# Issue order around the change of row tiles: a weight split ahead of the next rows' parts, merged quarter transfers, and an earlier turn of old rows

## The chip, the cores and the metric

The kernel runs on one core of one Trainium2 chip. The metric is the device time of one execution in microseconds (us). Engines are named as in the profile: PE is TensorE (matmuls), PEld its weight loads, DVE is VectorE, ACT is ScalarE, POOL is GpSimd, and SP is SyncE, which issues almost all of the DMAs here (SPq is its queue). PSUM is the memory that PE writes its results to, and SBUF the memory that all engines work in.

## What is computed

Eight batches of 576 tokens, eight heads of 64: two attention steps through 32 packed queries, a two-dimensional Fourier transform of which the real part is added, a normalisation, and a two-layer network with a relu. The part around which the change turns is the last one:

```python
p_packed = sm_attn(p, k, v)
x = sm_attn(q, p_packed, p_packed)           # then (8, 576, 512)
u = x + np.real(np.fft.fft(np.fft.fft(x, axis=1), axis=2))
un = (u - mu) / np.sqrt(var + 1e-06)
return u + np.maximum(un @ w_ch1, 0.0) @ w_ch2   # 512 -> 2048 -> 512
```

All is in 32-bit floating point. Each matrix product of the network is made of three matmuls of a faster 32-bit type: every operand is split into a high part (a rounding copy on ACT) and a low part (the rest, a subtraction), and the product is high x high + high x low + low x high.

## The kernel before

**Tiles.** The 4608 rows (8 x 576) are cut into 36 blocks of 128 rows, with the name key: (batch, "E" or "O", 0 or 1), and after each second batch a block of leftover rows "R". Four blocks make a tile of 512 rows, so there are nine tiles, 0 to 8. While the network runs on tile t, `front(t + 1)` computes the rows u of batch t + 1 in small steps between the network's matmuls; its last part ("rest") runs on into steps 0 and 2 of the next tile.

**The network of one tile (`ffn`, L643).** The 2048 hidden units are 16 slices, j = 0 to 15. `up(j)` is 12 matmuls (4 pieces of the inner dimension, three products each) into a PSUM tile ph; ACT then writes hh (relu, high part) and DVE hl (low part). `down(j)` is 12 matmuls (4 row blocks, three products each) which add into four PSUM tiles acc. The loop runs down one slice behind up: up(j), then down(j - 1); down(15) stands after the loop. Here a run of 12 matmuls is called a half step. `step(i)`, called twice a slice (i = 2j and 2j + 1), runs what falls due and the next piece of `front`.

**Weights and their splits.** All weights stay in SBUF (w1f, w2f). Each use splits 128x512 of them anew: `wsplits` (L633) is a generator, and each `next(splits)` issues one split, wr_h on ACT (L101) and wr_l on POOL (L102), and queues it in `ready`. Six buffers "wr" hold three splits. Two are issued in each j: the first is w1[j + 1], the second w2[j]; at j = 15 the first is w2[15], which down(15) reads, the second w1[0] for the next tile; one more, w1[1], follows down(15).

**The rows of the next tile (`Turned`, L581).** up reads the rows transposed and split, in one pair of tiles uh, ul (one buffer each, four quarters of 128 columns). `parts(i)` makes block i's quarter: a copy to uh on ACT and the subtraction to ul on DVE. As there is one buffer, parts can only run when up(15) has ended. At j = 15 parts(0) and parts(1) come behind up(15), parts(2) behind down(14), parts(3) behind down(15); the next up(0) reads all four. In its first slice the four matmuls with ul come last.

The turned rows that parts reads come by one of two ways, for each pair h of blocks (h = 0: blocks 0 and 1, h = 1: blocks 2 and 3), by `kind`:

- "late", where the block is finished too late in this tile: `less` on DVE, and `moves`, eight transposes on PE in among the matmuls of down(14) and down(15).
- "old" (both blocks belong to earlier batches) and "new" (a block of the batch now being computed): `less_quarters` subtracts the mean on ACT (un, L612), `turn` (L616) transposes 32x32 squares on DVE (flip, L619), and 16 DMAs on SP (raw, L623) put the squares in place. Each DMA moves 32 partitions of two blocks: two runs of 128 elements (512 B) a partition. un has two buffers ("ln").

Pairs into tiles 1, 2, 3 are new, late; into tiles 4, 5, 6, 7 old, new; into tile 8 old, old. Before, the first old pair is turned after step 24 (j = 12), and a new pair, or the second of two old pairs, at j = 13 (un behind down(12), the turn after step 27). At the end of a tile four DVE operations (L721) add acc into u, and four DMAs (L722) store it.

**What sets the order.** From tile 1 on (L769), the instructions of PE, DVE, ACT and POOL keep the order in which the program issues them. Tile 0's are ordered by a planner when the program is built, and so is SP's queue in all tiles. Each engine works through its instructions in order.

`statistics` puts squares (ACT, L208), a scalar operation (DVE, L211) and a power (POOL, L212) one and two steps behind a block.

Of the kernel before, what the change touches and what calls it, by code (L numbers as in the profile page):

```python
# [9 lines left out]
F32 = mybir.dt.float32  # L10
# [7 lines left out]
P = 128  # L18
# [61 lines left out]
def tile_kernel(ctx, tc, kpT, qT, v, w1, w2, tabs, tabR, tabB, tabT, sel, ident_d, out):  # L80
    nc = tc.nc
# [3 lines left out]
    ld = ctx.enter_context(tc.tile_pool(name="ld", bufs=2))  # L85
    work = ctx.enter_context(tc.tile_pool(name="work", bufs=2))
# [39 lines left out]
    def load_base():  # L126
        nc.gpsimd.dma_start(basis, tabB)
        nc.sync.dma_start(turn, tabT)
# [452 lines left out]
    class Turned:  # L581
# [32 lines left out]
                                     AF.Identity, bias=stat_of[key][:, 1:2], scale=1.0)  # L614

        def turn(self, h):  # L616
            flip = ld.tile([P, 2, 4, P], F32, tag="ld", name="flip")
            for n in range(2):
                nc.vector.transpose(flip[:, n].rearrange("p q x -> p (q x)"), self.un[2 * h + n])  # L619
            raw = work.tile([P, 2, 4, P], F32, tag="wst", name="raw", bufs=2)  # L620
            for a in range(4):
                for q in range(4):
                    nc.sync.dma_start(raw[32 * q:32 * (q + 1), :, a, :], flip[32 * a:32 * (a + 1), :, q, :])  # L623
            for n in range(2):
                self.tp[2 * h + n] = raw[:, n].rearrange("p q (c k) -> p q c k", c=4)

        def parts(self, i):
            if self.hl is None:
# [4 lines left out]
    def wsplits():  # L633

        for _ in tiles:
            for n, j in [(0, 0)] + [x for j in range(1, NJ) for x in ((0, j), (1, j - 1))] + [(1, NJ - 1)]:
                hi = work.tile([P, DM], F32R, tag="wr", name="wr_h", bufs=6)
                lo = work.tile([P, DM], F32R, tag="wr", name="wr_l", bufs=6)
                split(hi, lo, (w1f, w2f)[n][:, j, :], nc.gpsimd)
                ready.append((hi, lo))  # L640
                yield

    def ffn(first, turned, step, nxt, alone, following):  # L643
        keys = turned.keys
        n = len(keys)
        T = n * P
        uh, ul = turned.hl
        acc = [psf.tile([P, DM], F32, tag=f"acc{i}", name=f"acc{i}") for i in range(n)]
        now["acc"] = acc

        def up(j):
            wh, wl = ready.pop(0)

            pool, tag = (ps, "ps") if alone and j % 2 else (psf, "ph")
            ph = pool.tile([P, 512], F32, tag=tag, name="ph")

            step = T // 2 if first == 0 and j < SPL else T
            order = sorted(range(12), key=lambda k: k % 3 == 1) if j == 0 else range(12)
            for t in (slice(i, i + step) for i in range(0, T, step)):
                for n, k in enumerate(order):  # L660
                    c, (l, r) = k // 3, ((wh, uh), (wh, ul), (wl, uh))[k % 3]
                    nc.tensor.matmul(ph[:, t], l[:, c * P:(c + 1) * P], r[:, c, t], start=(n == 0), stop=(n == 11))  # L662
            hh = work.tile([P, 512], F32R, tag="hh", name="hh")
            hl = work.tile([P, 512], F32R, tag="hl", name="hl")
            nc.scalar.activation(hh[:, :T], ph[:, :T], AF.Relu)  # L665
            nc.vector.scalar_tensor_tensor(hl[:, :T], ph[:, :T], 0.0, hh[:, :T].bitcast(F32), ALU.max, ALU.subtract)  # L666
            return hh, hl

        def down(j, hh, hl, moves=()):

            moves = list(moves)
            vh, vl = ready.pop(0)
            for i in range(n):
                w = slice(i * P, (i + 1) * P)
                for k, (l, r) in enumerate(((hh, vh), (hh, vl), (hl, vh))):
                    nc.tensor.matmul(acc[i], l[:, w], r, start=(j == 0 and k == 0), stop=(j == NJ - 1 and k == 2))  # L676
                    if moves:
                        moves.pop(0)()

        kinds = [nxt.kind(h, following) for h in range(2)] if nxt else []  # L680
        assert kinds in ([], ["new", "late"], ["old", "new"], ["old", "old"]), kinds

        prev = None
        late = "late" in kinds
        for j in range(NJ):
            last = nxt is not None and j == NJ - 1
            cur = up(j)
            if last:
                if late:
                    nxt.less(2)  # L690
                    nxt.less(3)
                nxt.parts(0)
                nxt.parts(1)
            next(splits, None)
            step(2 * j)
            if j == 12:
                if kinds[:1] == ["old"]:
                    nxt.less_quarters(0)
                    nxt.turn(0)
            if prev is not None:  # L700
                down(j - 1, *prev, [lambda: None] * 8 + nxt.moves(2) if last and late else ())
                if j == 13:
                    for h in range(2):
                        if kinds and (h == 1 or kinds[h] != "old") and kinds[h] != "late":
                            nxt.less_quarters(h)
                if last:
                    nxt.parts(2)
                next(splits, None)
            step(2 * j + 1)
            if j == 13:  # L710
                for h in range(2):
                    if kinds and (h == 1 or kinds[h] != "old") and kinds[h] != "late":
                        nxt.turn(h)
            prev = cur
        down(NJ - 1, *prev, nxt.moves(3) if late else ())
        if nxt:
            nxt.parts(3)
        next(splits, None)
        for i, key in enumerate(keys):
            u = u_of[key]  # L720
            nc.vector.scalar_tensor_tensor(u, acc[i], stat_of[key][:, 2:3], u, ALU.mult, ALU.add)  # L721
            nc.sync.dma_start(out[(first + i) * P:(first + i + 1) * P, :], u)  # L722
            free.append(place_of[key])
# [24 lines left out]
    ready, splits = [], wsplits()  # L748
    next(splits)
    next(splits)  # L750
    for t, (first, tk) in enumerate(tiles):

        gen = front(t + 1) if t + 1 < B else iter(())
        ended = []

        def step(i):

            next_step()
            if t > 0 and i in (0, 2):
                next(rest, None)  # L760
            elif not ended and next(gen, None) == "rest":
                ended.append(gen)
            if t == 0 and i % 2 == 0 and i // 2 + LEAD < NJ:
                load_weights(i // 2 + LEAD)
            assert i < 2 * NJ - 1 or t + 1 >= B or ended

        nxt = Turned(tiles[t + 1][1]) if t + 1 < len(tiles) else None

        with tc.manual_schedule(engines=MANUAL) if t > 0 else nullcontext():  # L769
            ffn(first, cur, step, nxt, t + 1 >= B, t + 1)  # L770
        cur, rest = nxt, gen
# [112 lines left out]
```

## Time and profile before

| | us |
|---|---|
| median of three runs (1031.3, 1029.72, 1031.12) | 1031.12 |
| the profiled execution's own time | 1029.28 |
| one raw transfer, issue to landing | 1.9 |
| one copy to uh on ACT, median | 0.616 |
| one subtraction to ul on DVE, median | 0.688 |

The profile is of one execution, which was 1.84 us below the median. The page lists by engine what is busy and what chain of work ended last; "chain" rows called issue are time in which an engine waited for nothing that the profile shows. In a timeline a row gives the start in us, the duration, engine, line, operation, output <- input, and in brackets the idle time before it and what ended that. PE's matmuls are pipelined: a matmul of 512 columns shows 0.39 us, while its successor starts 0.227 us after it at full clock. A granted clock of 1.00 is full speed.

How the sixteen DMAs of a turn stand on SP, in the change from tile 5 to tile 6: first the 32 of both turns, then loads for a later batch.

```profile
704.85 20.82 SPq L623 DMA_DIRECT2D raw<-flip  x32
725.76 1.60 SPq L224 DMA_DIRECT2D kp<-kpT  x2
730.04 2.31 SPq L722 DMA_DIRECT2D out<-ubuf  x4
```

### The profile page before, as it was taken

Reading aid. Unit: us, or ns where it says so; the run is one execution under the profiler, and the core shown is the slowest. Engines: PE = TensorE matmul, PEld = TensorE weight load, DVE = VectorE, ACT = ScalarE, POOL = GpSimd, SP = SyncE. Lnnn points to the kernel's source line nnn. Section 1 sums busy time; section 2 is a strip of 40 time slices with the busy share of each in tenths; the row PEclk is TensorE's granted clock in tenths of the full one; section 3 lists DMA queues with packets and bytes.
Section 4 is the critical chain, followed back from the end, with each engine's and each line's share of the span. In section 5 each row is a group of like instructions: output and inputs, shape, how many; then the busy total and the mean of one; then the engine's idle time right before and its main releaser. Section 6 shows DMA issues by size and latency. Waiting matters only on the chain.

```text
span 1027.5 us, 15015 instructions
## 1 busy us (share of the span) xinstructions
PE 962.4 (94%) x5588; PEld 784.0 (76%) x5588; DVE 578.7 (56%) x1227; ACT 458.5 (45%) x936; POOL 473.6 (46%) x426
## 2 busy tenths in 40 slices
PE   4199889999999999999999999999999999997998
PEld 2177678778877887788777887788778888886886
DVE  4885863669455855587457845694558552122112
ACT  4578634444443444444544454445444442342322
POOL 3715634364345534454445434643454354443443
PEclk9599989999999999999999999999999999998999
DMA  9367301310042002300240024001410020011001
GB/s 361 116 181 269 124 1 45 107 57 1 9 130 71 1 1 86 99 1 1 79 150 1 1 61 139 31 1 28 156 47 1 18 66 1 1 29 54 1 1 41
DMA packets 34825, 65.93 MB, mean 64 GB/s; under 512 B 5494, under 2 KB 19648, under 8 KB 34752
## 3 DMA queue, kind: packets, MB, share of 16 engines
q1 hardware_dynamic: 33776, 63.53, 18.8%
q0 software_dynamic: 976, 1.44, 0.4%
q8 instruction: 44, 0.72, 0.3%
q14 instruction: 29, 0.24, 0.1%
HBM read 48.70 MB, written 9.44 MB: 57 GB/s over the span
## 4 chain that ended last, share of the span: by engine, by line
PE 65%; issue 8%; DVE 8%; SPq 7%; POOL 5%; ACT 4%; DMA 3%; POOLq 0%; ACTq 0%; DVEq 0%
PE ph L662 30%; PE acc L676 25%; SPq L623 7%; POOL wr_l L102 4%; DVE turned L410 1%; DVE turned L406 1%; PE po L317 1%; DMA raw<-flip 1%; PE s L260 1%; DMA wst<-w 1%; PE py L228 1%; PE py L230 1%; PE py L229 1%; PE e1tp L294 1%; DVE flip L619 1%
## 5 line engine op out<-in xcount | busy, mean ns | idle before, releaser
L102 POOL TENSOR_TENSOR wr_l<-w1f,wr_h 128x512 fp32r<-128x512 f32 x144 | 192.7, 1340 | 362.6 <-ACT wr_h L101 358.4
L666 DVE SCALAR_TENSOR_TENSOR hl<-ph,hh 128x512 fp32r<-128x512 f32 x144 | 98.9, 687 | 315.4 <-ACT hh L665 315.0
L102 POOL TENSOR_TENSOR wr_l<-w2f,wr_h 128x512 fp32r<-128x512 f32 x144 | 192.8, 1339 | 118.5 <-ACT wr_h L101 108.4
L662 PE MATMUL ph<-uh,wr_h 128*128 128x512 f32 (+1 forms) x580 | 230.9, 398 | 16.7 <-DVE hl L666 8.8
L676 PE MATMUL acc<-wr_l,hh 128*128 128x512 f32 x576 | 226.2, 393 | 5.8 <-POOL wr_l L102 5.8
L676 PE MATMUL acc<-wr_h,hh 128*128 128x512 f32 x576 | 226.5, 393 | 2.3 <-ACT wr_h L101 1.9
L662 PE MATMUL ph<-uh,wr_l 128*128 128x512 f32 (+1 forms) x580 | 227.5, 393 | 0.9 <-POOL wr_l L102 0.7
L676 PE MATMUL acc<-wr_h,hl 128*128 128x512 f32 x576 | 225.2, 391 | 0.0
L662 PE MATMUL ph<-ul,wr_h 128*128 128x512 f32 (+1 forms) x580 | 222.1, 391 | 0.0
L665 ACT ACTIVATE hh<-ph 128x512 fp32r<-128x512 f32 x144 | 86.0, 597 | 288.0 <-PE ph L662 287.7
L662 PEld LDWEIGHTS ph<-uh,wr_h 128*128 128x128 f32 x580 | 110.1, 190 | 52.3 <-DVE hl L666 10.2
L676 PEld LDWEIGHTS acc<-wr_l,hh 128*128 128x128 f32 x576 | 108.2, 188 | 29.7 <-POOL wr_l L102 8.6
L662 PEld LDWEIGHTS ph<-uh,wr_l 128*128 128x128 f32 x580 | 109.9, 189 | 25.8 <-POOL wr_l L102 2.4
L676 PEld LDWEIGHTS acc<-wr_h,hh 128*128 128x128 f32 x576 | 108.2, 188 | 25.7 <-ACT wr_h L101 3.4
L662 PEld LDWEIGHTS ph<-ul,wr_h 128*128 128x128 f32 x580 | 109.9, 190 | 22.3 <-DVE mx L279 0.8
L676 PEld LDWEIGHTS acc<-wr_h,hl 128*128 128x128 f32 x576 | 108.1, 188 | 22.8
L101 ACT CAST wr_h<-w1f 128x512 fp32r<-128x512 f32 x144 | 88.3, 613 | 10.7 <-PE acc L676 7.2
L101 ACT CAST wr_h<-w2f 128x512 fp32r<-128x512 f32 x144 | 89.1, 619 | 8.3 <-PE ph L662 6.7
L228 PE MATMUL py<-gh,fh 128*128 128x258 f32 x64 | 18.7, 294 | 27.5 <-ACT fh L470 27.5
L208 ACT ACTIVATE junk<-ubuf,stat 128x512 f32<-128x512 f32 x36 | 25.8, 720 | 36.4 <-DVE stat L204 36.4
L102 POOL TENSOR_TENSOR gl<-turned,gh 128x516 fp32r<-128x516 f32 x16 | 25.3, 1582 | 22.9 <-ACT gh L101 22.9
L228 PEld LDWEIGHTS py<-gh,fh 128*128 128x128 f32 x64 | 12.4, 194 | 28.5 <-ACT fh L470 28.0
(201 smaller groups left out, 1291.9 us busy)
## 6 DMA issues: line engine op xcount, KB each, us to landing
kp<-kpT SPq DMA_DIRECT2D x16, 608.0 KB, 4.0
out<-ubuf SPq DMA_DIRECT2D x36, 256.0 KB, 2.1
vt<-v SPq DMA_DIRECT2D x14, 640.0 KB, 4.7
wst<-w SPq DMA_DIRECT2D x17, 512.0 KB, 4.4
qt<-qT SPq DMA_DIRECT2D x14, 576.0 KB, 4.6
raw<-flip SPq DMA_DIRECT2D x208, 32.0 KB, 1.9
ubuf<-w SPq DMA_DIRECT2D x9, 512.0 KB, 3.7
w1f<-w SPq DMA_DIRECT2D x3, 512.0 KB, 14.0
```

Source lines behind the costliest of these rows:

```text
L101: nc.scalar.copy(hi, src)
L102: (lo_eng or nc.vector).tensor_tensor(lo, src, hi.bitcast(F32), ALU.subtract)
L208: nc.scalar.activation(junk, u, AF.Square, bias=st[:, 1:2], scale=1.0, accum_out=st[:, 2:3])
L228: nc.tensor.matmul(o, lh, rh, start=first, stop=False)
L229: nc.tensor.matmul(o, lh, rl, start=False, stop=False)
L230: nc.tensor.matmul(o, ll, rh, start=False, stop=last)
L260: nc.tensor.matmul(res[g][c][at, :w.stop - w.start], lhs(g, h), rhs(g, h, w), start=True, stop=True, tile_position=(r, h * NPK))
L623: nc.sync.dma_start(raw[32 * q:32 * (q + 1), :, a, :], flip[32 * a:32 * (a + 1), :, q, :])
L662: nc.tensor.matmul(ph[:, t], l[:, c * P:(c + 1) * P], r[:, c, t], start=(n == 0), stop=(n == 11))
L665: nc.scalar.activation(hh[:, :T], ph[:, :T], AF.Relu)
L666: nc.vector.scalar_tensor_tensor(hl[:, :T], ph[:, :T], 0.0, hh[:, :T].bitcast(F32), ALU.max, ALU.subtract)
L676: nc.tensor.matmul(acc[i], l[:, w], r, start=(j == 0 and k == 0), stop=(j == NJ - 1 and k == 2))
```

## The change

Three edits. (1) In each j, the first `next(splits)` is called ahead of the parts of the next tile instead of behind them; this makes a difference only at j = 15, where it is the split of w2[15]. (2) flip and raw are laid out with the quarter outside and the block inside, so that one quarter of two blocks is one run of 256 elements (1024 B) a partition in each DMA; there are still 16 DMAs a turn, and DVE writes each transposed block as four pieces. (3) Every old pair is now prepared and turned after step 22 (j = 11): the first old pair of tiles 3 to 7, from step 24; the second of tile 7, from j = 13. For new pairs nothing moves.

```diff
         def turn(self, h):
-            flip = ld.tile([P, 2, 4, P], F32, tag="ld", name="flip")
+            flip = ld.tile([P, 4, 2, P], F32, tag="ld", name="flip")
             for n in range(2):
-                nc.vector.transpose(flip[:, n].rearrange("p q x -> p (q x)"), self.un[2 * h + n])
-            raw = work.tile([P, 2, 4, P], F32, tag="wst", name="raw", bufs=2)
+                nc.vector.transpose(flip[:, :, n, :], self.un[2 * h + n].rearrange("p (q x) -> p q x", q=4))
+            raw = work.tile([P, 4, 2, P], F32, tag="wst", name="raw", bufs=2)
             for a in range(4):
                 for q in range(4):
-                    nc.sync.dma_start(raw[32 * q:32 * (q + 1), :, a, :], flip[32 * a:32 * (a + 1), :, q, :])
+                    nc.sync.dma_start(raw[32 * q:32 * (q + 1), a].rearrange("p n x -> p (n x)"),
+                                      flip[32 * a:32 * (a + 1), q].rearrange("p n x -> p (n x)"))
             for n in range(2):
-                self.tp[2 * h + n] = raw[:, n].rearrange("p q (c k) -> p q c k", c=4)
+                self.tp[2 * h + n] = raw[:, :, n, :].rearrange("p q (c k) -> p q c k", c=4)
...
             cur = up(j)
+            next(splits, None)
             if last:
                 if late:
                     nxt.less(2)
                     nxt.less(3)
                 nxt.parts(0)
                 nxt.parts(1)
-            next(splits, None)
             step(2 * j)
-            if j == 12:
-                if kinds[:1] == ["old"]:
-                    nxt.less_quarters(0)
-                    nxt.turn(0)
+            if j == 11:
+                for h in range(2):
+                    if kinds[h:h + 1] == ["old"]:
+                        nxt.less_quarters(h)
+                        nxt.turn(h)
             if prev is not None:
                 down(j - 1, *prev, [lambda: None] * 8 + nxt.moves(2) if last and late else ())
                 if j == 13:
                     for h in range(2):
-                        if kinds and (h == 1 or kinds[h] != "old") and kinds[h] != "late":
+                        if kinds[h:h + 1] == ["new"]:
                             nxt.less_quarters(h)
...
             if j == 13:
                 for h in range(2):
-                    if kinds and (h == 1 or kinds[h] != "old") and kinds[h] != "late":
+                    if kinds[h:h + 1] == ["new"]:
                         nxt.turn(h)
```

## The prediction

> **What bounds the kernel.** I read the page first, then TensorE's waits, then busy time and clock window by window around each change of tile, then the timelines of ACT, POOL and SP there.
>
> ```profile
> span 1027.5 us, 15015 instructions
> ...
> PE 962.4 (94%) x5588; PEld 784.0 (76%) x5588; DVE 578.7 (56%) x1227; ACT 458.5 (45%) x936; POOL 473.6 (46%) x426
> ...
> PE 65%; issue 8%; DVE 8%; SPq 7%; POOL 5%; ACT 4%; DMA 3%; POOLq 0%; ACTq 0%; DVEq 0%
> ```
>
> TensorE is busy 94% of the span and no other engine over 56%, so only what shortens TensorE's idle or slow time counts. Its longest waits:
>
> ```profile
> PE py L228 <- ACT fh L470: 27.5, 2, 26.0
> PE ph L662 <- DVE hl L666: 8.8, 4, 5.1
> PE ph L662 <- ACT uh L101: 5.9, 4, 4.5
> PE acc L676 <- POOL wr_l L102: 5.8, 7, 0.8
> ```
>
> (total, times, longest.) The first two belong to tile 0, which the change hardly touches. The last two are what it is about: rows of the next tile (uh) that come late, and the remainder of a weight split (wr_l) that comes late at seven changes of tile. I now measure each change. "Change 6-7" is the end of tile 6 and the start of tile 7. Columns: window, length, TensorE busy (instructions, with one or two that reach over an edge), granted clock, DMA share, GB/s.
>
> ```profile
> 179.73:186.13 6.40, 6.40 (x34) 1.00 0.01 4
> 286.90:295.50 8.60, 6.94 (x33) 1.00 0.32 86
> 396.35:405.11 8.76, 6.93 (x34) 1.00 0.28 83
> 505.97:516.63 10.66, 9.06 (x37) 1.00 0.36 108
> 614.74:625.42 10.68, 9.08 (x38) 1.00 0.35 104
> 723.47:733.22 9.75, 8.81 (x38) 1.00 0.67 234
> 831.31:840.60 9.29, 8.46 (x38) 1.00 0.17 57
> 921.89:941.81 19.92, 14.51 (x49) 0.83 0.23 76
> 919.17:921.89 2.72, 2.72 (x13) 1.00 0.22 56
> 928.60:933.10 4.50, 0.01 (x1) 0.93 0.11 29
> 933.10:939.00 5.90, 5.80 (x13) 0.50 0.48 178
> ```
>
> The ninth row is the ruler: a half step (12 matmuls) at full pace takes 2.72 us. Rows 1 to 3 (changes 0-1, 1-2, 2-3) hold down(14), down(15) and eight transposes; rows 4 to 7 hold down(14), down(15) and the next up(0), 3 x 2.72 = 8.16 at full pace; row 8 (change 7-8) holds down(14), down(15), up(0), up(1), 10.88. Change 0-1 stands without a stall, at 6.40. The excess is 8.60 - 6.40 = **2.20**, 8.76 - 6.40 = **2.36**, then **2.50**, **2.52**, **1.59**, **1.13**, and 19.92 - 10.88 = **9.04**: together **21.34 us**. The last two rows show why change 7-8 costs so much: 4.5 us idle, then 5.9 us at half clock.
>
> **The change, part by part.**
>
> *The split ahead of the parts.* ACT at change 7-8, then POOL and TensorE:
>
> ```profile
> 922.09 0.60 ACT L665 ACTIVATE hh<-ph 128x512 fp32r<-128x512 f32 x1 [3.82 <-PE ph L662]
> 922.58 1.13 ACT L101 CAST uh<-raw 128x512 fp32r<-128x512 f32 x2
> 923.62 0.62 ACT L101 CAST wr_h<-w2f 128x512 fp32r<-128x512 f32 x1
> ```
> ```profile
> 924.31 1.46 POOL L102 TENSOR_TENSOR wr_l<-w2f,wr_h 128x512 fp32r<-128x512 f32 x1 [3.92 <-ACT wr_h L101]
> ```
>
> The split of w2[15] stands behind two uh copies, so wr_l ends at 925.77. Down(15) would reach its second matmul, which reads it, at 921.89 + 2.72 + 0.23 = 924.84. Issued first, wr_h starts at 922.58 and wr_l ends about 924.6, in time. In changes 1-2 and 2-3 it is worse, as the uh copies wait for their transfers and hold the split. That the order is what counts, change 0-1 shows, where wr_h was issued ahead:
>
> ```profile
> 177.04 0.62 ACT L101 CAST wr_h<-w2f 128x512 fp32r<-128x512 f32 x1 [1.60 <-PE acc L676]
> ...
> 180.78 1.13 ACT L101 CAST uh<-raw 128x512 fp32r<-128x512 f32 x2
> ```
>
> So this part takes all of 2.20, 2.36 and 1.13, and by the same 1.13 of each of the four others: 5.69 + 4 x 1.13 = **10.2 us**. In return uh0, uh1, their ul, and in changes 1-2 to 6-7 the pow pair on POOL behind them come 0.52 us later; the split takes the wr buffers of w2[13], read out half a step before, so it adds no wait. Next late is then wr_l of w1[0], the pair of POOL instructions being ahead of it:
>
> ```profile
> 509.81 1.06 POOL L212 TENSOR_TENSOR stat<-stat,mhalf 128x1 f32<-128x1 f32 x2
> ```
>
> At change 3-4 I lay it out: uh1 ends 508.3, ul1 509.2, the scalar pair on DVE 509.3, L212 510.4, wr_l (1.3 us) 511.75; up(0) asks for it at 505.97 + 5.44 + 0.23 = 511.64. With its hand-over that is 0.15 us left at each of changes 3-4 to 6-7 (0 to 0.5): **-0.6**. In changes 1-2 and 2-3 the transposes give TensorE 0.9 us more, and nothing is left.
>
> *One run per transfer.* SP's issue durations (ns, least/median/most) of today's two-run transfers and of a load with one run a partition:
>
> ```profile
> L623 SPq DMA_DIRECT2D raw<-flip x208: 585/595/1257, 160.3 to 929.4; - x104
> ```
> ```profile
> L224 SPq DMA_DIRECT2D kp<-kpT x16: 327/334/530, 0.7 to 727.0; - x16
> ```
> ```profile
> 908.88 21.11 SPq L623 DMA_DIRECT2D raw<-flip  x32
> ```
> ```profile
> raw<-flip SPq DMA_DIRECT2D x208, 32.0 KB, 1.9
> ```
>
> 32 issues take 21.11 us, 0.66 each. With one run of 1024 B instead of two of 512 B an issue costs between 0.33 (kp, a load from HBM) and 0.60 us (unchanged), plus 0.06 between issues; I take 0.34, as its pattern is kp's: 16 issues 6.4 us instead of 10.2 to 10.6. DVE's turn writes four pieces instead of one: at most its 0.7 us again, and DVE is under 60% busy. The sum needs this part little, since the next one starts the transfers early enough; what it is worth at the other end stands under rival A. The Trainium skill, "DMA: Bandwidth & Descriptors", Specifications, puts line rate at 512 B a descriptor and above, which the old runs have already: by that rule merging gains nothing in the transfer itself, and only SP's issue time could move.
>
> *Old pairs at step 22.* In tile 7 both old pairs now start at step 22. Today the 32 transfers run from 908.88; the last lands at 931.4, and TensorE stands:
>
> ```profile
> 931.44 0.62 ACT L101 CAST uh<-raw 128x512 fp32r<-128x512 f32 x1 [7.20 <-DMA raw<-flip]
> ```
>
> One loop turn earlier (5.44 us) the first goes out at 903.5, the last at 903.5 + 32 x 0.4 = 916.3, landed by 918.2, before up(15) ends at 921.89. Then uh2 and uh3 run right behind uh1, wr_l of w1[0] is done about 926.6, and up(0) starts at 927.33 without a gap. The half clock goes with the gap: after tile 0's wait of 5.1 us for hl, which ended at 132.88 (second wait row), the clock halves in the same way, while stalls of 1 us (rows 2 to 7 above) leave 1.00:
>
> ```profile
> 132.90:137.00 4.10, 4.10 (x10) 0.50 0.00 0
> ```
>
> Of 9.04 this part gets 7.91 beside the split's 1.13. The slow stretch alone cost 941.81 - 933.15 - 5.44 = 3.2 us. The Trainium skill, "TensorE: Matmul & The Clock Gate", Part 1, gives about 3.4 us of cold pace after an idle window of 3.4 us; by that estimate the slow stretch is 1.7 us and the sum 1.5 smaller. The trace has it longer, and is used.
>
> In tiles 3 to 6 the old pair's turn moves likewise, past nothing on SP but the kp load that stood between the two turns:
>
> ```profile
> 499.03 0.33 SPq L224 DMA_DIRECT2D kp<-kpT  x1
> 499.42 10.48 SPq L623 DMA_DIRECT2D raw<-flip  x16
> ```
> ```profile
> 511.40 0.62 ACT L101 CAST uh<-raw 128x512 fp32r<-128x512 f32 x1 [3.10 <-DMA raw<-flip]
> ```
>
> That load went out only when the first turn had landed, and held the second turn (its flips were done at 497.5) by 1.9 us. Now the first turn has landed before 493. The second runs 497.6 + 16 x 0.4 + 1.9 = 505.9, before uh2 can start (508.2). So the rest of 2.50, 2.52 and 1.59 goes: 1.37 + 1.39 + 0.46 = 3.22.
>
> What the move costs: ACT's two un copies and DVE's flips, each moved ahead of the split of w2[11]:
>
> ```profile
> 906.77 1.34 ACT L612 ACTIVATE un<-ubuf,stat 128x512 f32<-128x512 f32 x2
> ```
> ```profile
> 907.53 1.33 DVE L619 STREAM_TRANSPOSE flip<-un 128x512 f32<-128x512 f32 x2 [0.44 <-ACT un L612]
> ```
> ```profile
> 905.80 0.39 PE L676 MATMUL acc<-wr_l,hh 128*128 128x512 f32 x1
> ```
>
> In tiles 3 to 6 down(11) lies behind other matmuls, over 5 us later: free. In tile 7 four un copies stand there, and the third waits for the first flip (two ln buffers): un from 901.33, third 902.85, fourth to 904.2, wr_h to 904.7, wr_l to 906.1, asked for at 905.80: **-0.3** (0 to 0.6).
>
> **Sum:** 21.34 - 0.6 - 0.3 = 20.4 us. The profiled execution took 1029.28 (span 1027.5): 1008.9. The median shown, 1031.12, lies 1.84 above it: **1010.7 us**.
>
> **Rivals.**
>
> *A, transfers no cheaper to issue.* For it: the two-run and one-run rows differ in more than the runs (SBUF to SBUF against HBM). Then 32 x 0.66 from 903.5 end at 924.6, land at 926.5; uh2, wr_h, wr_l follow to 929.1, 1.2 us after up(0) asks. At 3-4 and 4-5 wr_l of w1[0] moves to 512.2, 0.55 each. Together 2.3: 1013.0.
>
> *B, the gap at 7-8 stays long enough for half clock,* SP holding the second old pair back behind something its planner puts there. Against it: SP has nothing but raw and the final stores in that stretch. 3.2 us for the clock with a gap of 2 or more, up to all 7.9: 1016 to 1018.6.
>
> *C, the split's move does not act,* since POOL or the hh copy is the limit: 10.2 come back, 1020.9. Change 0-1 speaks against it.
>
> *D, slower.* Tile 0 is the one whose order on the engines is planned when the program is built, not written out; the new order and the new transfer shape lie in it. Its plan has a 27.5 us wait for fh already (first wait row). If the new plan makes tile 0 over 20.4 us longer, the whole is slower; a second wait like that one gives 1010.7 + 27.5 = 1038. Against it: the changed instructions stand after 159 us, behind that wait, with 30 us of tile 0 left.
>
> **How the numbers follow.** Forecast 0.66 (own range 1008.5 to 1012.3: the residues from 0 to 2 + 0.6, the runs' spread), A 0.17, B 0.07, C 0.05, D 0.05. The range 1007.5 to 1016.0 takes in the forecast, A and the near end of B. A measurement here tells about 0.2% (2 us) from none. Faster by more than that: forecast, A, B and C, 0.95, less 0.01 for an unforeseen mixture; within 0.2%: 0.02, a D that just cancels; slower: 0.04.
>
> **What would show it.** POOL wr_l and ACT uh gone from TensorE's waits at changes of tile; windows as above at 6.4, 8.2 to 8.4 and 10.9 us; raw issues of about 335 ns; the clock at 1.00 after tile 7; a wait of 0.3 us for wr_l in down(11) of tile 7. I am wrong if a raw issue still takes 0.59 us, if uh waits for raw, if tile 0 lasts longer, or if the pow pair leaves over 0.5 us a change.

## The result, and the profile after

| | before | after |
|---|---|---|
| median of 4 runs (us) | 1031.1 (1029.72 to 1031.3) | 1018.46 (1017.34 to 1019.64) |
| ratio, with its 95% interval | | 0.988 (0.9863 to 0.9898) |
| profiled execution (its span) | 1029.28 (1027.5) | 1017.34 (1015.6) |

The change saves 12.6 us of the 20.4 that were forecast. The time lies 7.8 us above the forecast and 2.5 us above the upper end of the range.

From the page of the kernel after, span, busy times, and the shares of the chain that ended last:

```profile
span 1015.6 us, 15016 instructions
...
PE 957.9 (94%) x5588; PEld 782.3 (77%) x5588; DVE 582.9 (57%) x1227; ACT 459.2 (45%) x936; POOL 474.6 (47%) x426
...
PE 71%; DVE 8%; issue 7%; POOL 5%; ACT 3%; SPq 3%; DMA 2%; DVEq 0%; POOLq 0%; ACTq 0%
```

TensorE still sets the time, and SP's share of the chain fell from 7% to 3%: most of the time that the transfers had on the path is gone, as meant. TensorE's waits after (total, times, longest), of those that belong to changes of tile:

```profile
PE ph L663 <- POOL wr_l L102: 4.6, 5, 1.5
...
PE untp L603 <- DVE un L596: 1.6, 2, 0.8
...
PE ph L663 <- ACT uh L101: 0.5, 1, 0.5
...
PE acc L677 <- POOL wr_l L102: 0.2, 1, 0.2
```

The wait of down for wr_l (5.8 us before) is gone (the 0.2 left is a new place, in tile 7), that of up for uh fell from 5.9 to 0.5. In their place stand two new ones: up waits 4.6 us for a wr_l, and the transposes of moves wait 1.6 us for un, which is DVE's mean subtraction in `less`. POOL's wr_l is late again, one operation further on.

The windows of TensorE at changes 0-1 to 7-8, cut at the same instructions as the prediction's (start, end, length, busy time, clock, DMA share, GB/s):

```profile
180.01:186.41 6.40, 6.40 (x34) 1.00 0.01 4
287.13:294.58 7.45, 6.63 (x33) 1.00 0.33 97
395.47:402.90 7.43, 6.61 (x33) 1.00 0.33 97
503.74:513.75 10.01, 8.47 (x37) 1.00 0.56 185
611.91:620.98 9.07, 8.72 (x37) 1.00 0.35 108
719.03:728.54 9.51, 8.49 (x37) 1.00 0.56 190
826.67:836.64 9.97, 8.48 (x37) 1.00 0.34 121
918.43:929.83 11.40, 11.22 (x49) 1.00 0.30 106
```

At full pace they are three times 6.40, four times 8.16, and 10.88 long. What is over that is the excess. In the table it is worked out in this way for the profiled execution of each kernel (us). The kernels below the first two are those of the experiments. Change 0-1 is 0.00 or -0.01 in all of them and left out:

| kernel | 1-2 | 2-3 | 3-4 | 4-5 | 5-6 | 6-7 | 7-8 | sum |
|---|---|---|---|---|---|---|---|---|
| before | 2.20 | 2.36 | 2.50 | 2.52 | 1.59 | 1.13 | 9.04 | 21.34 |
| after | 1.05 | 1.03 | 1.85 | 0.92 | 1.35 | 1.81 | 0.52 | 8.52 |
| split_early | 0.01 | 0.01 | 0.37 | 1.15 | 0.76 | 0.05 | 0.21 | 2.56 |
| less_early | 0.01 | 0.01 | 1.87 | 1.09 | 1.70 | 1.57 | 0.33 | 6.58 |
| pow_late | 1.02 | 1.04 | 0.38 | 1.31 | 0.13 | 0.13 | 0.24 | 4.24 |
| half_issue | 1.03 | 1.04 | 1.38 | 1.35 | 1.39 | 1.38 | 0.20 | 7.77 |
| wide_issue | 1.03 | 1.04 | 1.36 | 1.37 | 1.39 | 1.38 | 0.22 | 7.78 |
| only_split | 1.04 | 1.04 | 4.95 | 3.25 | 1.78 | 1.75 | 8.68 | 22.48 |
| only_step22 | 2.20 | 3.93 | 1.65 | 1.12 | 1.67 | 1.09 | 1.10 | 12.75 |
| only_layout | 2.00 | 2.18 | 2.07 | 2.69 | 1.11 | 1.66 | 7.44 | 19.14 |
| early_pow | 0.01 | 0.01 | 0.41 | 1.09 | 0.00 | 0.50 | 0.51 | 2.52 |
| early_pow_half | 0.01 | 0.01 | 0.00 | 0.00 | 0.00 | 0.00 | 0.00 | 0.02 |

The excess fell by 12.8 us, and the span by 11.9, where 20.4 was forecast. The prediction left 0.6 us of the excess; 8.52 stayed. So 7.9 of the 8.5 us that the span misses lie at the changes of tile, in two kinds: about 1.04 at each of 1-2 and 2-3, and 0.9 to 1.85 at each of 3-4 to 6-7. The half clock behind change 7-8 is gone.

### What the two kinds of wait look like

Change 1-2, timelines after, of POOL, DVE and TensorE (start, duration, and in brackets the idle time before it and what ended that):

```profile
288.52 1.30 POOL L102 TENSOR_TENSOR wr_l<-w2f,wr_h 128x512 fp32r<-128x512 f32 x1 [2.88 <-ACT wr_h L101]
```
```profile
288.57 1.93 DVE L596 TENSOR_SCALAR un<-ubuf,stat 128x512 f32<-128x512 f32 x2
```
```profile
290.16 0.33 PE L603 MATMUL untp<-ident,un 128*128 128x128 f32 x1 [0.82 <-DVE un L596]
```

And DVE and POOL in the kernel before, where this split came later:

```profile
288.34 0.87 DVE L596 TENSOR_SCALAR un<-ubuf,stat 128x512 f32<-128x512 f32 x2
```
```profile
291.11 1.34 POOL L102 TENSOR_TENSOR wr_l<-w2f,wr_h 128x512 fp32r<-128x512 f32 x1 [5.71 <-ACT wr_h L101]
```

The same two un operations take 0.87 us before and 1.93 after, though DVE waits for no result. They start 0.05 us after POOL's wr_l. The split that was moved ahead now lies on them, and the second column is where this is seen: an instruction got longer, and no view calls it a wait.

Change 3-4, timelines after, of DVE, POOL, ACT and TensorE:

```profile
505.59 1.98 DVE L102 TENSOR_TENSOR ul<-raw,uh 128x512 fp32r<-128x512 f32 x2 [0.33 <-ACT uh L101]
507.50 0.20 DVE L211 TENSOR_SCALAR stat<-stat 128x1 f32<-128x1 f32 x2
507.69 0.69 DVE L102 TENSOR_TENSOR ul<-raw,uh 128x512 fp32r<-128x512 f32 x1
508.73 0.69 DVE L102 TENSOR_TENSOR ul<-raw,uh 128x512 fp32r<-128x512 f32 x1 [0.35 <-ACT uh L101]
```
```profile
505.12 1.30 POOL L102 TENSOR_TENSOR wr_l<-w2f,wr_h 128x512 fp32r<-128x512 f32 x1 [2.88 <-ACT wr_h L101]
507.71 2.11 POOL L212 TENSOR_TENSOR stat<-stat,mhalf 128x1 f32<-128x1 f32 x2 [1.29 <-DVE stat L211]
509.80 2.53 POOL L102 TENSOR_TENSOR wr_l<-w1f,wr_h 128x512 fp32r<-128x512 f32 x2
```
```profile
507.56 0.62 ACT L101 CAST wr_h<-w1f 128x512 fp32r<-128x512 f32 x1
```
```profile
509.20 0.39 PE L663 MATMUL ph<-uh,wr_h 128*128 128x512 f32 x1
511.12 0.50 PE L663 MATMUL ph<-uh,wr_l 128*128 128x512 f32 x1 [1.53 <-POOL wr_l L102]
```

Read it as a chain. POOL's wr_l of w2[15] starts at 505.12; the two ul beside it take 1.98 us, where two take 1.28 below in split_early. So the scalar pair L211 ends at 507.70. The pow pair L212 starts at 507.71 together with the next ul, its second half runs beside the last ul, and it takes 2.11 us, where the prediction's row had 1.06. Only then comes wr_l of w1[0], and up(0) waits 1.53 us for it. The two stretches are 0.70 + 1.05 = 1.75 us; without them that wr_l would, by estimate, end near 509.5 (wr_h ends at 508.18, and 1.3 on top), just when up(0) asks for it with its second matmul, 0.23 us after its first, at 509.43.

**The theory** from this: DVE and POOL hold each other up in SBUF. An un, or a ul from raw, that starts on DVE while wr_l runs on POOL stands until that wr_l ends, and a power that starts on POOL behind a ul stands until the ul ends. The Trainium skill, "SBUF — State Buffer", Who interferes with whom, states such a rule: the port pair that the two engines share is an exclusive lock, held for a whole instruction, and a DVE operation takes part if it runs in a two-port mode or has both inputs in SBUF. The trace agrees, with 0.87 against 1.93, 1.28 against 1.98 and 1.06 against 2.11 us; in which mode un runs it does not say. In one case it does not agree: at change 4-5 of the kernel after, a ul that starts while the second power runs is not held up.

```profile
615.88 1.06 POOL L212 TENSOR_TENSOR stat<-stat,mhalf 128x1 f32<-128x1 f32 x2 [1.29 <-DVE stat L211]
```
```profile
616.45 0.69 DVE L102 TENSOR_TENSOR ul<-raw,uh 128x512 fp32r<-128x512 f32 x1 [0.59 <-ACT uh L101]
```

The rule spoke against the move, and the prediction did not weigh it.

**The rivals:** that the transfers are at fault (SP's issues did not get cheaper, the prediction's rival A), or only the order on POOL's queue (the pow pair ahead of wr_l, with no stretch).

### The profile page after: what moved, and what is told of

Its sections match the earlier page's. It is cut to its first block, busy times and chain, and to the rows that moved or that the text cites. A ratio compares the mean times of both kernels' runs of the same rounds, so it can differ in the third digit from the quotient of the medians.

```text
span 1015.6 us, 15016 instructions
## 1 busy us (share of the span) xinstructions
PE 957.9 (94%) x5588; PEld 782.3 (77%) x5588; DVE 582.9 (57%) x1227; ACT 459.2 (45%) x936; POOL 474.6 (47%) x426
## 4 chain that ended last, share of the span: by engine, by line
PE 71%; DVE 8%; issue 7%; POOL 5%; ACT 3%; SPq 3%; DMA 2%; DVEq 0%; POOLq 0%; ACTq 0%
PE ph L663 32%; PE acc L677 28%; POOL wr_l L102 3%; SPq L623 3%; DVE turned L410 1%; PE po L317 1%; PE s L260 1%; DVE turned L406 1%; ACT hh L666 1%; PE py L228 1%; PE py L230 1%; PE py L229 1%; PE e1tp L294 1%; DMA ubuf<-w 1%; PE pz L228 1%
## 5 line engine op out<-in xcount | busy, mean ns | idle before, releaser
L212 POOL TENSOR_TENSOR stat<-stat,mhalf 128x1 f32<-128x1 f32 x36 | 25.1, 707 | 30.8 <-DVE stat L211 30.6
```

The lines of the kernel that those rows point to most:

```text
L212: nc.gpsimd.tensor_tensor(st[:, 2:3], st[:, 2:3], mhalf, ALU.pow)
```

## The experiments

### First set: one obstacle at a time

split_early: the split goes one half step further ahead, so that wr_l is over before un and ul start.

```diff
+            if last:
+                next(splits, None)
             cur = up(j)
-            next(splits, None)
+            if not last:
+                next(splits, None)
```

> The changed kernel, with the split of w2[15] issued ahead of up(15) instead of behind it. Port theory (DVE operations with two SBUF inputs or of the un kind and POOL operations wait for each other, so the moved wr_l now stands in the way of un and ul): wr_l is over before un and ul start; un takes 0.87 us for two again instead of 1.93, the PE wait for un (0.8 us at changes 1-2 and 2-3) goes, ul of blocks 0 and 1 takes 1.28 instead of 1.98, and the excess of changes 3-4 to 6-7 falls from 5.9 us together to about 2. Total 4 to 6 us less than the changed kernel. Transfer theory (the rows come late because a raw issue still takes 0.59 us): uh of block 2 still waits for raw, and the total falls by less than 1 us.

Measured: median 1013.14 us (1011.77 to 1014.73), ratio to before 0.9836 (0.9812 to 0.9861); that interval lies below that of the kernel after (0.9863 to 0.9898). DVE and POOL at change 3-4:

```profile
505.15 1.28 DVE L102 TENSOR_TENSOR ul<-raw,uh 128x512 fp32r<-128x512 f32 x2
```
```profile
503.32 1.30 POOL L102 TENSOR_TENSOR wr_l<-w2f,wr_h 128x512 fp32r<-128x512 f32 x1 [1.11 <-ACT wr_h L101]
506.57 1.06 POOL L212 TENSOR_TENSOR stat<-stat,mhalf 128x1 f32<-128x1 f32 x2 [1.95 <-DVE stat L211]
508.25 3.02 POOL L102 TENSOR_TENSOR wr_l<-w1f,wr_h 128x512 fp32r<-128x512 f32 x2 [0.61 <-ACT wr_h L101]
```

And un at change 1-2, with the window of that change:

```profile
289.91 0.87 DVE L596 TENSOR_SCALAR un<-ubuf,stat 128x512 f32<-128x512 f32 x2
```
```profile
288.48:294.89 6.41, 6.41 (x33) 1.00 0.37 113
```

The instructions that the theory named (un, the first two ul, the pow pair) are back at their short durations, the windows 1-2 and 2-3 stand at full pace, and the excess falls from 8.52 to 2.56. One stretch is new: the last ul of 3-4 now starts beside wr_l of w1[0] and takes 1.38 us, and the two wr_l take 3.02 where the kernel after has 2.53; the change loses only 0.37 us. SP's issues are what they were. Both stalls come from where the moved split lies against DVE's work.

less_early: only the un operations are moved, ahead of up(15), out from under wr_l.

```diff
+            if last and late:
+                nxt.less(2)
+                nxt.less(3)
             cur = up(j)
             next(splits, None)
             if last:
-                if late:
-                    nxt.less(2)
-                    nxt.less(3)
```

> The changed kernel, with the two un operations of late pairs (DVE) ahead of up(15) instead of behind it, so that they do not meet wr_l of w2[15] on POOL. Port theory: the excess of changes 1-2 and 2-3 (1.05 and 1.03 us) goes to about 0, changes 3-4 to 7-8 stay: 2 us less than the changed kernel. Transfer theory: nothing moves, as the transfers are as they were.

Measured: 1017.94 us (1016.44 to 1018.53), ratio 0.9881 (0.9861 to 0.99). The excess of 1-2 and 2-3 is gone (1.05 and 1.03 to 0.01), that of 3-4 to 7-8 is not. In the profiled execution that is 2.1 us at the two changes; the medians differ by only 0.5 us from the kernel after, with overlapping intervals, so that alone it can't be told from no gain in the time.

pow_late: only the scalar and pow pair (L211, L212) of the blocks whose key ends in 1 is put four steps later, behind wr_l of w1[0] on POOL.

```diff
-        after(2, deviation)
+        after(6 if key[1] != "R" and key[2] == 1 else 2, deviation)
```

> The changed kernel, with the scalar operation on DVE and the power on POOL of the last two blocks of each batch four steps later, so that they no longer stand ahead of wr_l of w1[0] at the end of a tile. Port theory with the POOL queue: the waits for wr_l of w1[0] at changes 3-4 to 6-7 go (excess 5.9 us together to 1.5 or less), changes 1-2 and 2-3 keep about 1 us each: 4 to 4.5 us less than the changed kernel. Transfer theory: less than 1 us.

Measured: 1014.05 us (1013.66 to 1014.79), ratio 0.9846 (0.9828 to 0.9864). The mirror image of less_early: 1-2 and 2-3 keep 1.02 and 1.04, 3-4 to 6-7 fall from 5.93 together to 1.95. So the two kinds of wait are two places of one cause: un under wr_l at the first two, and ul, pow pair, wr_l in a row at the others. Taking the pair out of the row helps as much as taking the stretch out, so queue order on POOL matters too; but without the stretches the row costs little (0.37 us at 3-4 against 1.85), as split_early shows with the pair left in it.

half_issue: half as many transfers, of 2048 B a partition instead of 1024. The squares then land in places that the reference does not want.

```diff
-                for q in range(4):
+                for q in range(2):
-                    nc.sync.dma_start(raw[32 * q:32 * (q + 1), a].rearrange("p n x -> p (n x)"),
-                                      flip[32 * a:32 * (a + 1), q].rearrange("p n x -> p (n x)"))
+                    nc.sync.dma_start(raw[32 * a:32 * (a + 1), 2 * q:2 * q + 2].rearrange("p a n x -> p (a n x)"),
+                                      flip[32 * (3 - a):32 * (4 - a), 2 * q:2 * q + 2].rearrange("p a n x -> p (a n x)"))
```

> The changed kernel with 8 transfers a turn of 2048 B a partition instead of 16 of 1024 B: the same bytes and half the issues; the squares are put in other places than the computation wants. Transfer theory: the second turn lands 5 us earlier, uh no longer waits for raw, and the excess of changes 3-4 to 6-7 goes: 4 to 6 us less than the changed kernel. Port theory: uh comes earlier, but wr_l of w1[0] still stands behind the pow pair, which still waits for DVE: less than 1.5 us.

Measured: 1018.12 us (1016.51 to 1018.63), ratio 0.9882 (0.9863 to 0.9901), excess 7.77 against 8.52. With half of the issues the time stays. As the kernel after stands, the transfers are not what its time hangs on; what is left at each of 3-4 to 6-7 (1.35 to 1.39) is the row of DVE and POOL, now the same at every change. SP's issue durations (ns, least/median/most) of raw, in the kernel after and in this one:

```profile
L623 SPq DMA_DIRECT2D raw<-flip x208: 507/589/1756, 160.6 to 919.9; - x104
```
```profile
L623 SPq DMA_DIRECT2D raw<-flip x104: 507/589/1672, 160.3 to 908.2; - x104
```

The median is 589 with one run (595 before, with two), and 589 with twice the bytes. The prediction took 340.

### Second set: each part of the change alone, and what an issue costs

only_split: the kernel before, with the split ahead of the parts and nothing else.

```diff
             cur = up(j)
+            next(splits, None)
             if last:
...
-            next(splits, None)
```

> The kernel before with the first edit alone (the split of w2[15] ahead of the parts). The prediction's account (parts add up): 10.2 us less than before. Port theory, with the late transfers of before still there: changes 1-2 and 2-3 fall to about 1.05 us of excess each, 3-4 to 7-8 keep theirs within 0.6, since uh and the pow pair are then what is late: 2 to 3.5 us less than before.

Measured: 1030.42 us over 10 runs (1028.81 to 1036.39), ratio 1.001 (0.9991 to 1.0028): no gain, and not the 2 to 3.5 us that the port theory gave it either. The wait of up for uh, 5.9 us before, is now

```profile
PE ph L662 <- ACT uh L101: 11.5, 4, 6.2
```

The 2.50 and 2.52 us that 3-4 and 4-5 lost to wr_l and uh together became 4.95 and 3.25: uh waits for its transfers, whoever is ahead of it. At 3-4 of this profiled execution the last two transfers also landed late, 3.0 us after their issue, where the same two took 1.9 before (DMA view of 505.9 to 509.5):

```profile
q8 instruction: 1, 0.02, 2.0%
...
raw<-flip SPq DMA_DIRECT2D x2, 32.0 KB, 3.0
```

The first row is a load of instructions, one packet of 16 KB, which the kernel before had 1.3 us later against the start of the change, when the last transfer was all but landed. That it held the two up is inferred from the coincidence. So about 1 us of the 4.95 is not the split's own. The gap also cost the clock (windows from the start of the gap):

```profile
508.80:511.29 2.49, 0.03 (x1) 1.00 0.31 51
511.29:513.00 1.71, 1.38 (x4) 0.88 0.74 295
513.00:515.00 2.00, 2.00 (x6) 0.50 0.42 157
```

only_step22: the kernel before, with both old pairs turned after step 22 and nothing else (the last three hunks of the diff, with the old layout and the old place of the split).

```diff
-            if j == 12:
-                if kinds[:1] == ["old"]:
-                    nxt.less_quarters(0)
-                    nxt.turn(0)
+            if j == 11:
+                for h in range(2):
+                    if kinds[h:h + 1] == ["old"]:
+                        nxt.less_quarters(h)
+                        nxt.turn(h)
```

> The kernel before with the third edit alone (old pairs turned after step 22, old layout). The prediction's account: 21.34 - 10.2 - 0.3, about 11 us less than before, the seven waits for wr_l of w2[15] staying. Port theory: change 7-8 falls from 9.04 to about 1.5, 3-4 to 6-7 to 1.1 to 1.5 each, 1-2 and 2-3 stay at 2.2 and 2.36: 10 us less than before.

Measured: 1021.29 us (1019.48 to 1023.33), ratio 0.9916 (0.9896 to 0.9935), 9.7 us below the median of before beside it (1031.01). This part alone is most of the gain; change 7-8 falls from 9.04 to 1.10. Change 2-3 rose from 2.36 to 3.93, by a stretch of half clock that the last section shows.

only_layout: the kernel before, with the new flip, raw and transfers of `turn`, and nothing else (the first hunk of the diff).

```diff
-            flip = ld.tile([P, 2, 4, P], F32, tag="ld", name="flip")
+            flip = ld.tile([P, 4, 2, P], F32, tag="ld", name="flip")
...
-                    nc.sync.dma_start(raw[32 * q:32 * (q + 1), :, a, :], flip[32 * a:32 * (a + 1), :, q, :])
+                    nc.sync.dma_start(raw[32 * q:32 * (q + 1), a].rearrange("p n x -> p (n x)"),
+                                      flip[32 * a:32 * (a + 1), q].rearrange("p n x -> p (n x)"))
```

> The kernel before with the second edit alone (one run of 1024 B instead of two of 512 B). If a second run costs issue time, the median raw issue falls to about 0.34 us, the second turns land 4 us and more earlier, and the total falls by 5 us or more. If not, the issue stays near 0.59 us and the total within 1 us of before.

Measured: 1028.84 us over 10 runs (1026.39 to 1030.14), ratio 0.9988 (0.9974 to 1.0002). If it gains, it is by some 2 us, and the interval takes in no gain. Its issues have the same median of 589 ns as the kernel after.

wide_issue: 16 transfers over all 128 partitions, 256 B each, with the squares in places that the reference does not want.

```diff
-            for a in range(4):
-                for q in range(4):
-                    nc.sync.dma_start(raw[32 * q:32 * (q + 1), a].rearrange("p n x -> p (n x)"),
-                                      flip[32 * a:32 * (a + 1), q].rearrange("p n x -> p (n x)"))
+            to, of = (t.rearrange("p a n x -> p (a n x)") for t in (raw, flip))
+            for i in range(16):
+                nc.sync.dma_start(to[:, 64 * i:64 * (i + 1)], of[:, 64 * i:64 * (i + 1)])
```

> The changed kernel with 16 transfers a turn of 128 partitions and 256 B each instead of 32 partitions and 1024 B: the same bytes, the same number of issues, SBUF to SBUF; the squares stay in the places the computation doesn't want. If the 32 partitions make an issue cost 0.59 us, it falls to about 0.33 as with the loads; if SBUF to SBUF makes it, it stays at 0.5 to 0.6.

Measured, in one run: 1017.4 us, and

```profile
L623 SPq DMA_DIRECT2D raw<-flip x208: 465/599/1841, 160.7 to 919.8; - x104
```

Neither runs, nor bytes, nor partitions move the issue from 0.59 us. What the four forms share, and kp with its 0.33 does not, is that both ends lie in SBUF. That this is the reason is inferred; no run changes it alone.

### Third set: both obstacles away, then the transfers too

early_pow is split_early and pow_late together. It computes the same as the kernel after.

> The changed kernel with both: the split of w2[15] ahead of up(15), and the pow pair of the last two blocks four steps later. Port theory: both obstacles gone, the excess of changes 1-2, 2-3, 3-4, 5-6, 6-7 and 7-8 falls to 0.4 us or less each; change 4-5 keeps about 1.1, where uh itself waits for the transfers. Sum 2 us against 2.6 (split ahead alone) and 4.2 (pow later alone): 0.3 to 1 us less than with the split ahead alone, about 6 less than the changed kernel. If the two remedies were worth what each was alone, they would add to 10 us less than the changed kernel.

Measured: 1012.32 us (1011.28 to 1012.88), ratio 0.982 (0.9806 to 0.9835). Its interval lies wholly below that of the kernel after (0.9863 to 0.9898): this is a version that beats both kernels, by 18.3 us against before (1030.59 in that set). It does not beat split_early alone by what the intervals can tell, and the excess is 2.52 against 2.56: the further 0.3 to 1 us that was expected did not show, and 6-7 and 7-8 keep 0.50 and 0.51 where 0.4 or less was. At 4-5, which keeps 1.09, one issue took 1.38 us in place of 0.59, and its transfer landed after 2.6 us in place of 1.9.

early_pow_half is early_pow with half_issue's transfers, squares misplaced as there.

> The same with 8 transfers a turn of 2048 B a partition instead of 16; the squares are put in other places than the computation wants. If what is left at change 4-5 is the transfers, it falls from about 1.1 us of excess to 0.3 or less, and the sum to under 1 us: 1 us less than with 16 transfers. If it is not the transfers, nothing moves.

Measured: 1009.66 us (1007.68 to 1010.29), ratio 0.979 (0.9773 to 0.9808). Two of its windows, at 3-4 and 7-8:

```profile
502.70:510.86 8.16, 8.16 (x37) 1.00 0.35 134
...
911.40:922.28 10.88, 10.88 (x49) 1.00 0.26 96
```

No change of tile costs anything any more. Idle time ahead of the instructions on uh that ended when a transfer landed (us, times), in early_pow:

```profile
  DMA raw<-flip: 11.1, 7
```

In early_pow_half no such row is left. In the kernel after it is 7.3 us (19.5 before), and in half_issue it is gone. So the transfers were late all the time, but hidden behind the row of DVE and POOL: half_issue on top of the kernel after took 0.75 us of excess away, on top of early_pow 2.50. Together with the 6.0 that the two reorderings take (8.52 to 2.52) this accounts for all 8.52.

## Why the prediction was off, step by step

- **The split ahead of the parts.** Its direct effect came: down(15)'s wait for wr_l is gone at all seven changes. The step that failed is the price in return, "0.15 us left at each of changes 3-4 to 6-7", and "nothing is left" at 1-2 and 2-3. These were sized by shifting the operations by 0.52 us with the durations that they had before. The durations changed, because the moved wr_l came to lie on un and ul: 1.05 + 1.03 + 5.93 + 0.52, or 8.5 us, stayed instead of 0.6. By the experiments 6.0 of that are DVE and POOL in each other's way, and 2.5 the transfers.
- **One run per transfer.** An issue was taken at 0.34 us "as its pattern is kp's"; it measured 0.589, the upper end of the stated bounds. Rival A had this right in its premise, and it priced the lateness at 2.3 us, near the 2.5 that early_pow and early_pow_half show. That nearness is partly luck: A put 1.2 at 7-8 and 0.55 each at 3-4 and 4-5, where early_pow keeps 0.51, 0.41 and 1.09, and 0.50 at 6-7. In the kernel itself little of that is seen, since the other chain ended later.
- **Old pairs at step 22.** Held: 7-8 fell from 9.04 to 0.52, the clock in that window is 1.00, and the part alone is worth 9.7 us, where 11.1 less 0.3 was forecast.
- **Down(11) of tile 7** waits as forecast, 0.17 us for wr_l at 902.17 where 0.3 was taken.
- **Adding the parts.** In the sum the split part was 10.2 us and stood by itself. Alone it gained nothing that can be measured; on top of the other two it is at most the 2.9 us by which the gain of the whole (12.6) exceeds that of only_step22 (9.7). Where wr_l and uh are late together, removing one shows the other. How much of that is so in only_split is not settled, since the late landing at 3-4 and the half clock behind it are in its time.
- **Rivals B, C and D.** B did not come. C's 1020.9 lies 2.4 us from the time measured, nearer than the forecast, but that is luck: its mechanism (the move does not act) is refuted, as the move acts, and makes a new stall. D did not come: tile 0 ends at 186.41 instead of 186.13 in the profiled execution.

With the two obstacles and the dear issues out of the way, early_pow_half, which leaves the squares in wrong places, reaches 1009.66, close to the forecast of 1010.7. The goal was right, and the path to it had two more obstacles than the prediction saw. Three of the signs of being wrong that it named came: the issue at 0.59 us, uh waiting for raw, and over 0.5 us a change behind the pow pair. One hint stood in the trace of before, in the durations of ul (ns, least/median/longest), first from raw in SBUF, then from untp in PSUM:

```profile
L102 DVE TENSOR_TENSOR ul<-raw,uh x26: 680/688/1378, 181.5 to 933.1; 128x512 fp32r<-128x512 f32 x26
L102 DVE TENSOR_TENSOR ul<-untp,uh x10: 678/692/692, 62.8 to 404.1; 128x512 fp32r<-128x512 f32 x10
```

With two inputs in SBUF the longest takes twice the median; with one in PSUM there is no such tail. Four of the 26 took 1.36 to 1.38 us, and each of them started beside a wr_l on POOL; the five ul from PSUM that did so took 0.69.

**What stays open:** what only_split would gain without the late landing, why the load of instructions comes when it does, and whether only_layout gains anything. The end of tile 0 alone lay between 185.8 and 189.1 us in the profiled executions, with the same order on the engines there (but for two matmuls that change places in only_layout), so single profiles can't settle differences of 2 us; the windows at the changes of tile can, since each is cut at its own instructions.

## What to carry to other kernels

Before an operation is moved on one engine, look at what runs at its new time on the engine that shares a resource with it, and price the move with the durations of overlapping pairs, not of lone ones; the least, median and longest duration of a line show in the old trace whether the operation has such a second duration. A stall that another one covers is worth nothing until both are gone, so edits that aim at one place are to be priced together. A smaller issue cost is taken from a row with the same two ends (here SBUF to SBUF), not from one with the same shape.

## What the runs showed of the hardware that was not expected

- A pow on 128x1 elements, two of which take 1.06 us alone, takes 2.11 us for two beside two ul on DVE: a tiny POOL instruction is held up as a large one is. The other way round it is not so: a ul behind a pow takes its 0.69 us.
- The issue of a SBUF to SBUF transfer on SP took a median of 0.589 to 0.599 us for 256, 1024 and 2048 B a partition, and 32 or 128 partitions.
- The clock halves after shorter gaps than the 4.5 us of the kernel before: in only_split after 2.49 us (windows above), and in only_step22 at change 2-3 after waits of 0.99 and 0.83 us close together. Yet a gap of 2.27 us in only_split at 4-5 left it at 1.00, and so did the lone wait of 1.53 us at 3-4 of the kernel after. The traces show what tells these apart. The granted clock changes only at the edges of slots of 3.41 us, which run on through an execution, and it follows how busy TensorE was in the slot before. Windows cut at these slots, from only_split (the gap of 2.49 us, with the half clock behind it shown above, and the gap of 2.27 us), only_step22 (the two waits, the slot behind them) and the kernel after (the lone wait):

```profile
509.16:512.57 3.41, 0.95 (x3) 1.00 0.56 174
618.39:621.80 3.41, 1.73 (x8) 1.00 0.26 42
```
```profile
401.87:405.29 3.42, 1.67 (x8) 1.00 0.60 182
405.29:408.70 3.41, 3.41 (x10) 0.50 0.07 23
```
```profile
509.61:513.02 3.41, 1.90 (x8) 1.00 0.78 298
```

TensorE was busy for 0.28 and 0.49 of the two slots that half clock followed, and for 0.51 and 0.56 of the two that it did not. In all twelve profiled executions, from 60 us on, each slot at full clock with a busy share up to 0.39 was followed by half clock and none from 0.50 up was; of seven slots between 0.43 and 0.49 three were. So a gap counts by where it lies in the slots: the 2.27 us lay across an edge. The Trainium skill, "TensorE: Matmul & The Clock Gate", Part 1, names an idle window of about 3.4 us; here a slot of that length that was busy for half of it was enough.
